# A Nyström attention, GLU and soft-MoE kernel on one Trainium2 core: idle products, the last soft-MoE's tiles and the prefetch ring changed

## The chip, the core and the metric

The kernel runs on one core of one Trainium2 chip. The metric is the device time of one execution in microseconds. The kernel before was timed in three runs: 731.29, 730.26 and 728.56 us, a median of 730.26 us. Times in rows are counted from the start of the profiled execution's span.

## What is computed

Three layers follow each other, all in float32 at the inputs and outputs. `B, H, S, D = 8, 8, 576, 64`, 4608 tokens of 512 features.

```python
# 1 Nystroem attention, per batch and head, 32 landmarks
A, Bm, C = softmax(q @ k_lm.T), softmax(q_lm @ k_lm.T), softmax(q_lm @ k.T)
Z = six Newton steps from Bm.T / (norm1 * norminf)
x = A @ Z @ C @ v
# 2 GLU
x = (silu(x @ w_gate) * (x @ w_val)) @ w_out
# 3 soft MoE, 8 experts with 4 slots each
logits = x @ phi                                   # (4608, 32)
d = softmax(logits, over tokens); slot_input = d.T @ x
for e in range(8):
    slot_out[e] = relu(slot_input[e] @ w1[e]) @ w2[e]
c = softmax(logits, over slots)
out = c @ slot_out
```

## The kernel before, in words

The whole work is written for one core with a tile framework that places instructions on the engines (PE, DVE, ACT, POOL, and SP for DMAs), follows the dependences of tiles, and orders each engine's instructions. The kernel walks over 8 batches. Each batch has 12 column blocks of the GLU (`unit`, line 880), and beside these the attention of the next batch (`attention`) and the soft-MoE of the batch before (`softmoe(b)`, line 778, a generator in steps) run in slots that a table of numbers gives.

`softmoe(b)` takes the batch's logits L from PSUM into the tile LT (128 x 160: 576 tokens as 4 x 144, so the last 32 columns are used on 64 partitions only). It finds the maximum over tokens of each slot (`cm`, a transpose `m_x` on PE, `gm`, `gmax`, `row`), spreads it with a product `m_y`, takes the exponential of LT with the sum of its rows (`dsum`), transposes LT to DN, spreads DN by four products `m_dr` (line 834) into DR, and multiplies DR with the GLU's result HB in 72 small products `m_d` (line 848), which four DVE operations add to Sacc. The running sum over tokens is `den`. A second copy of the logits, CN, becomes the softmax over slots.

For batch 7, the last, no GLU runs beside it. There `keep_warm` (line 770) puts products on PE whose result nobody reads: 3, 4, 2 and 2 of them (`WARM`, line 911) at four places, with LT or DN as stationary operand.

After the loop the tail (lines 1086 to 1212) follows: `m_s` transposes Sacc, `m_si` multiplies it with w_out (three tiles `wo`, read back from DRAM) to the experts' input SI, a transpose `m_sit` and twelve copies (lines 1119 to 1126, half on DVE, half on ACT) write it three times into the operands ZP, the first expert products `m_f` (line 1156) read w1, the second (line 1204) w2, in two halves `dh` of the columns, and `outputs` multiplies with c, evicts to buffers `ob` and stores.

The experts' weights are 32 tiles of 1 MB (0 to 15 of w1, 16 to 31 of w2), all loaded by SP in order into a ring of buffers `ffn_tags` (line 980): seven buffers `fw` in the space that the attention leaves at the end of batch 6 (`tail_loads`, line 1001), three parts of HB, six tiles `w0` to `w5` of the GLU's weights (of which `w0` to `w2` first hold `wo`), and three buffers `fx` in the space that the GLU leaves. That makes 20. The seven `fw` are loaded at the last slot of batch 6; tile 16 goes into a part of HB when m_d of batch 7 has read it, 17 to 19 into `w0` to `w2` as `m_si` reads them, and tile 20 and the following each into the buffer that a product has just read (`pump`).

Of the kernel before, what the change touches and what calls it, by code (L numbers as in the profile page):

```python
# [18 lines left out]
M = 32  # L19
# [36 lines left out]
def nystrom_softmoe_kernel(  # L56
# [49 lines left out]
    DN = cp.tile([128, 5, M], F32, name="DN")  # L106

    DR = cp.tile([128, 4, 5, M], F32, name="DR")
    dsum = cp.tile([128, 2], F32, name="dsum")
    gmax = cp.tile([1, M], F32, name="gmax")  # L110
# [658 lines left out]

    def keep_warm(x, n):  # L770

        m = psp.tile([128, 512], F32, tag="pg", name="warm", bufs=2)
        for _ in range(n):
            pe.matmul(m[:, 0:160], ident, x, start=True, stop=True)

    mb_t = []

    def softmoe(b):
        L = L_t[b]
        assert ("l", b, NJ - 1) in seq  # L780
        act.copy(LT[:, 0:128], L[:, 0:128])
        act.copy(LT[0:64, 128:160], L[0:64, 128:160])
        yield
        cm = smp.tile([128, 2], F32, tag="cm", name="cm")
        dve.tensor_reduce(cm[:, 0:1], LT[:, 0:128], axis=AX.X, op=ALU.max)
        dve.tensor_reduce(cm[0:64, 1:2], LT[0:64, 128:160], axis=AX.X, op=ALU.max)
        dve.tensor_tensor(out=cm[0:64, 0:1], in0=cm[0:64, 0:1], in1=cm[0:64, 1:2], op=ALU.max)
        c = CN[:, b]
# [4 lines left out]
        if b == nb - 1:  # L793
            keep_warm(LT, WARM[0])
        row = smp.tile([1, 4, M], F32, tag="row", name="row")
# [17 lines left out]
        yield  # L813
        in_order("exp", LT[:, 0:128], LT[:, 0:128], AF.Exp, bias=mb[:, 0:1], accum_out=dsum[:, 0:1])
        in_order("exp", LT[0:64, 128:160], LT[0:64, 128:160], AF.Exp, bias=mb[0:64, 0:1], accum_out=dsum[0:64, 1:2])
        if b == nb - 1:
            keep_warm(LT, WARM[1])
        al = smp.tile([128, 1], F32, tag="al", name="al")
# [4 lines left out]
        dve.transpose(DN, LT.rearrange("p (k r) -> p k r", r=32))  # L823
        ds_ = smp.tile([128, 1], F32, tag="ds", name="ds")
        if b:
            dve.tensor_tensor(out=ds_, in0=dsum[:, 0:1], in1=dsum[:, 1:2], op=ALU.add)
            dve.scalar_tensor_tensor(out=den, in0=den, scalar=al, in1=ds_, op0=ALU.mult, op1=ALU.add)
        else:
            dve.tensor_tensor(out=den, in0=dsum[:, 0:1], in1=dsum[:, 1:2], op=ALU.add)
        yield  # L830

        for g in range(4):
            m = psp.tile([128, 512], F32, tag="x", name="m_dr", bufs=3)
            pe.matmul(m[:, 0:160], msum[32 * g:32 * g + 32, :], DN[32 * g:32 * g + 32].rearrange("p k s -> p (k s)"),
                      start=True, stop=True)
            o = DR[:, g].rearrange("p k s -> p (k s)")
            act.copy(o, m[:, 0:160]) if g % 2 else dve.tensor_copy(o, m[:, 0:160])
        if b == nb - 1:
            keep_warm(DN.rearrange("p k s -> p (k s)"), WARM[2])
        yield  # L840
# [10 lines left out]
        if b == nb - 1:  # L851
            keep_warm(DN.rearrange("p k s -> p (k s)"), WARM[3])
        yield
# [56 lines left out]

    WARM = [3, 4, 2, 2]

# [4 lines left out]
    pool.memset(one, 1.0)  # L917
    for t in (LT, dsum):
        pool.memset(t, 0.0)
    load_qk(0, 0)  # L920
# [57 lines left out]
    last = nb - 1  # L978
    NW, NX = 7, 3
    ffn_tags = ([f"fw{i}" for i in range(NW)] + ["00", "01", "02", "w3", "w4", "w5"] + [f"fx{i}" for i in range(NX)]  # L980
# [5 lines left out]
    def wbuf(tag, name):  # L986
        if tag[:2] in ("fw", "fx"):
            return (fwp if tag[1] == "w" else fxp)[0].tile([128, 2048], F32, tag=tag, name=name)
        return big(tag, name) if tag[0] == "w" else part(int(tag[0]), int(tag[1]))
# [105 lines left out]
    ST, SI = misc[:, 1408:1792].rearrange("p (i x) -> p i x", i=3), misc[:, 1792:1920]  # L1095
    act.copy(ST, m[:, 0:384].rearrange("p (i x) -> p i x", i=3))
    rden = smp.tile([128, 1], F32, name="rden")
    dve.tensor_scalar(rden, m[:, 384:385], 1e-9, None, ALU.add)
# [19 lines left out]
    mz = m[:, 0:128].rearrange("p (c j g s) -> p c j g s", c=4, j=4, g=2)  # L1118
    for a in range(3):
        for g in range(2):  # L1120
            for z, c in ((ZP3, slice(0, 3)), (ZP1, slice(3, 4))):
                o = z[:, :, 4 * g:4 * g + 4, 8 * a + 4 * g:8 * a + 4 * g + 4]
                if g:
                    act.copy(o, mz[:, c, :, g, :])
                else:
                    dve.tensor_copy(o, mz[:, c, :, g, :])

    cT = {}

    def c_split(b):  # L1130

        if b % 2 == 0:
            cT[b // 2] = wbuf(ffn_tags[12 + b // 2], f"cT{b // 2}").bitcast(F32R)[:, 0:2 * S]
        c3 = misc[:, 768:1408].bitcast(F32R).rearrange("p (k j a x) -> p k j a x", k=5, j=4, a=4)
# [35 lines left out]

    free = ffn_tags[16:] + ffn_tags[0:4]
    nob = [0]
# [24 lines left out]
    for dh in range(2):  # L1197
        m = psp.tile([128, 512], F32, tag="pg", name="m_f2", bufs=2)
        for g in range(2):
            for r in range(4):  # L1200
# [6 lines left out]
                if dh == 0 and 4 * g + r < nb:  # L1207
                    c_split(4 * g + r)
        SR = fxp[0].tile([128, 256], F32R, name=f"SR{dh}")
        act.activation(SH, m[:, 0:256], AF.Copy, scale=hi_sign)  # L1210
# [58 lines left out]
```

## Time and profile before

| what | value |
|---|---|
| median of three runs | 730.26 us |
| lowest, highest | 728.56, 731.29 us |
| the profiled execution: its time | 733.54 us |
| its span, first to last instruction | 731.8 us |
| mean granted clock of PE | 0.954 of 2.4 GHz |
| busy: PE, DVE, ACT, POOL | 664.4, 513.5, 318.1, 114.7 us |
| DMA: moved, mean rate | 105.04 MB, 144 GB/s |

A busy time is an average over stages that have different limits. The page cuts the span into 40 slices of 18.3 us; the windows cut it where a stage begins. PEclk is the share of PE's full clock that was granted. A granted clock of 0.50 is 1.2 GHz, of 1.00 it is 2.4 GHz.

### The profile page before, as it was taken

How to read it: one execution, taken by the hardware profiler on the slowest of the kernel's cores; microseconds unless marked ns; L12 is line 12 of the kernel's file. 1: busy time of each engine (PE TensorE's matmuls, PEld its weight loads, DVE VectorE, ACT ScalarE, POOL GpSimd, SP SyncE). 2: the span in 40 equal slices, each digit the busy share in tenths (PEclk: the TensorE clock that was granted, in tenths of full speed). 3: DMA queues.
4: the chain of work that ended last, by engine and by line, in shares of the span. 5: the costliest groups of instructions: out<-in, count | busy, mean ns of one | idle time of the engine just before them, and what ended most of it. 6: DMA issues, size and time to landing. Idle time of an engine off the chain costs nothing.

```text
span 731.8 us, 18736 instructions
## 1 busy us (share of the span) xinstructions
PE 664.4 (91%) x7749; PEld 488.8 (67%) x7749; DVE 513.5 (70%) x1247; ACT 318.1 (43%) x821; POOL 114.7 (16%) x125
## 2 busy tenths in 40 slices
PE   5687878999899999999999999999999998898990
PEld 1564657776587777767776777787768777662560
DVE  5999998878765896689578856985786655520351
ACT  2566766436433643364237333633453342301440
POOL 0544464302100120021012001200120000010000
PEclk9797898999999999999999999999999999979995
DMA  8687555204210330034011401240101699549999
GB/s 295 213 312 291 206 197 203 93 2 130 67 66 2 130 105 29 22 111 131 1 66 67 131 1 66 67 130 2 65 2 60 212 267 303 174 146 335 348 364 330
DMA packets 59990, 105.04 MB, mean 144 GB/s; under 512 B 3968, under 2 KB 29696, under 8 KB 58368
## 3 DMA queue, kind: packets, MB, share of 16 engines
q1 hardware_dynamic: 59904, 103.84, 43.5%
q8 instruction: 61, 1.00, 0.6%
q14 instruction: 25, 0.20, 0.1%
HBM read 91.24 MB, written 12.58 MB: 142 GB/s over the span
## 4 chain that ended last, share of the span: by engine, by line
PE 72%; DVE 14%; DMA 4%; ACT 4%; issue 2%; POOL 1%; SPq 0%; DVEq 0%; ACTq 0%; POOLq 0%
PE pg L877 20%; PE pv L877 18%; PE g L709 6%; PE l L761 5%; PE m_d L848 4%; PE m_n L636 3%; PE m_f L1156 2%; PE m_f L1204 2%; PE m_a L528 2%; DMA q<-in_qT_dram 2%; DMA out_dram<-ob 1%; DMA HB<-in_w_cat_dram 1%; PE m_c L528 1%; DVE bd L311 1%; PE m_v L617 1%
## 5 line engine op out<-in xcount | busy, mean ns | idle before, releaser
L301 ACT ACTIVATE u<-pg 128x288 f32<-128x288 f32 x174 | 71.5, 412 | 156.5 <-PE pg L877 146.8
L906 DVE TENSOR_TENSOR hT<-u,pv 128x288 f32<-128x288 f32 x162 | 72.9, 451 | 54.8 <-PE pv L877 48.6
L877 PE MATMUL pg<-EH,GH 128*128 128x288 f32 x384 | 97.9, 332 | 2.2 <-ACT GH L732 2.2
L877 PE MATMUL pv<-EH,GH 128*128 128x288 f32 x384 | 92.3, 314 | 3.9 <-DVE hT L906 3.9
L877 PE MATMUL pg<-EH,GL 128*128 128x288 f32 x384 | 87.5, 302 | 2.2 <-issue 2.0
L746 DVE TENSOR_TENSOR GL<-g,GH 128x512 fp32r<-128x512 f32 (+1 forms) x114 | 63.2, 580 | 34.1 <-ACT GH L732 33.7
L877 PE MATMUL pg<-EL,GH 128*128 128x288 f32 x384 | 84.8, 302 | 0.0
L877 PE MATMUL pv<-EH,GL 128*128 128x288 f32 x384 | 84.3, 296 | 0.0
L877 PE MATMUL pv<-EL,GH 128*128 128x288 f32 x384 | 83.4, 298 | 0.0
L877 PEld LDWEIGHTS pg<-EH,GH 128*128 128x128 f32 x384 | 61.0, 192 | 24.3 <-issue 19.0
L877 PEld LDWEIGHTS pv<-EH,GH 128*128 128x128 f32 x384 | 62.2, 190 | 21.4 <-issue 16.6
L766 DVE STREAM_TRANSPOSE HB<-hT 128x576 f32<-128x576 f32 x96 | 74.0, 770 | 1.6 <-POOL hT L902 0.2
L732 ACT CAST GH<-g 128x512 fp32r<-128x512 f32 (+1 forms) x114 | 51.7, 506 | 51.7 <-PE g L709 51.6
L877 PEld LDWEIGHTS pg<-EH,GL 128*128 128x128 f32 x384 | 63.5, 191 | 4.9 <-issue 3.6
L877 PEld LDWEIGHTS pg<-EL,GH 128*128 128x128 f32 x384 | 62.6, 192 | 2.5 <-issue 2.5
L877 PEld LDWEIGHTS pv<-EH,GL 128*128 128x128 f32 x384 | 62.8, 190 | 0.0
L877 PEld LDWEIGHTS pv<-EL,GH 128*128 128x128 f32 x384 | 62.7, 191 | 0.0
L709 PE MATMUL g<-w,WB 64*32 64x512 f32 (+1 forms) x976 | 59.7, 515 | 1.6 <-ACT HB L728 0.8
L761 PE MATMUL l<-hT,P_sb 128*32 128x128 f32 (+1 forms) x768 | 48.5, 301 | 0.6 <-DVE hT L906 0.6
L761 PEld LDWEIGHTS l<-hT,P_sb 128*32 128x32 f32 x768 | 16.1, 108 | 40.6 <-issue 17.6
L682 POOL TENSOR_TENSOR AN<-AN,mxA 128x576 f32<-128x576 f32 x16 | 18.4, 1167 | 152.9 <-DVE mxA L681 136.8
L848 PE MATMUL m_d<-HB,DR 32*32 32x384 f32 x1152 | 41.3, 513 | 0.0
(259 smaller groups left out, 1068.5 us busy)
## 6 DMA issues: line engine op xcount, KB each, us to landing
k<-in_kT_dram SPq DMA_DIRECT2D x52, 288.0 KB, 3.9
ffn<-in_w_dram SPq DMA_DIRECT2D x13, 1024.0 KB, 9.2
ffn<-in_w_dram SPq DMA_DIRECT2D x24, 512.0 KB, 8.8
HB<-in_w_cat_dram SPq DMA_DIRECT2D x8, 1024.0 KB, 6.1
v<-in_v_dram SPq DMA_DIRECT2D x8, 1024.0 KB, 5.6
q<-in_qT_dram SPq DMA_DIRECT2D x28, 288.0 KB, 3.5
HB<-in_w_out_dram SPq DMA_DIRECT2D x12, 512.0 KB, 5.3
out_dram<-ob SPq DMA_DIRECT2D x6, 1024.0 KB, 10.0
```

The source lines that it names most:

```text
L301: i = act.activation(*a, **kw)
L528: pe.matmul(ms[r][32 * hp:32 * hp + 32, 0:HALF], lm[64 * r:64 * r + 64, hp, :], qk_t[nm, b, hp][64 * r:64 * r + 64, HALF * half:HALF * hal ...
L636: pe.matmul(m[:, 96 * q:96 * q + 96], bd[:, q, :], RV[:, q, :], start=True, stop=True)
L682: lambda q: pool.tensor_tensor(out=AN[q], in0=AN[q], in1=bc[q], op=ALU.subtract),
L709: pe.matmul(gs[r][32 * hp:32 * hp + 32, 0:256 * n].rearrange("p (u f) -> p u f", u=n), WB[b % 2][64 * r:64 * r + 64, hp, :], w[64 * r:64 * ...
L732: act.copy(H_, g)
L746: dve.tensor_tensor(out=GL, in0=g, in1=GH, op=ALU.subtract)
L761: pe.matmul(L[32 * c:32 * c + 32, 0:32 * k], P_sb[:, j, :], main[:, 0:k, c, :], start=j == 0, stop=j == NJ - 1)
L766: dve.transpose(HB[b % 2][:, S * j:S * j + S].rearrange("p (t r) -> p t r", r=32), hT[:, 0:S].rearrange("p (t r) -> p t r", r=32))
L848: pe.matmul(ms[a][32 * g:32 * g + 32, 0:384].rearrange("p (j f) -> p j f", j=NJ), DR[32 * a:32 * a + 32, g, k, :], hb[32 * a:32 * a + 32, ...
L877: pe.matmul(ps[:, 0:HALF], G_t[b, j, q, sel_][h], e[:, q, ts_], start=n == 0, stop=n == 5)
L906: dve.tensor_tensor(out=o, in0=u, in1=pv[:, 0:HALF], op=ALU.mult)
```

## The change

It has seven edits.

1. `keep_warm` multiplies the constants (the identity with a part of `cst`) in place of LT or DN, into the PSUM buffer of the logits. The counts are 3, 5, 2, 2, and a fifth place, after the copy of `m_s`, has 2.
2. The corner of LT that holds no tokens is set to -3e38 by POOL in each `softmoe`, so that one maximum and one exponential run over the whole tile; `dsum` has one column, and the two additions with it are gone.
3. DR has no tile of its own any more; it lies in the unused end of the other HB.
4. The ring of weight tiles has eight `fw` buffers, 21 in all.
5. The copies into ZP write all three replicas at once, from an operand that is read three times: four on DVE, then four on ACT.
6. SR lies in buffer `w2` and no longer in the space of `fx`.
7. The buffers of the transposed c and of the outputs are taken from other places of the ring.

```diff
-    DR = cp.tile([128, 4, 5, M], F32, name="DR")
-    dsum = cp.tile([128, 2], F32, name="dsum")
+    dsum = cp.tile([128, 1], F32, name="dsum")
...
-    def keep_warm(x, n):
-        m = psp.tile([128, 512], F32, tag="pg", name="warm", bufs=2)
+    def keep_warm(n):
+        m = psp.tile([128, 512], F32, tag="l", name="warm")
         for _ in range(n):
-            pe.matmul(m[:, 0:160], ident, x, start=True, stop=True)
+            pe.matmul(m[:, 0:160], ident, cst[:, 128:288], start=True, stop=True)
...
-        yield
-        cm = smp.tile([128, 2], F32, tag="cm", name="cm")
-        dve.tensor_reduce(cm[:, 0:1], LT[:, 0:128], axis=AX.X, op=ALU.max)
-        dve.tensor_reduce(cm[0:64, 1:2], LT[0:64, 128:160], axis=AX.X, op=ALU.max)
-        dve.tensor_tensor(out=cm[0:64, 0:1], in0=cm[0:64, 0:1], in1=cm[0:64, 1:2], op=ALU.max)
+        pool.memset(LT[64:128, 128:160], -3e38)
+        yield
+        cm = smp.tile([128, 1], F32, tag="cm", name="cm")
+        dve.tensor_reduce(cm, LT, axis=AX.X, op=ALU.max)
...
-        in_order("exp", LT[:, 0:128], LT[:, 0:128], AF.Exp, bias=mb[:, 0:1], accum_out=dsum[:, 0:1])
-        in_order("exp", LT[0:64, 128:160], LT[0:64, 128:160], AF.Exp, bias=mb[0:64, 0:1], accum_out=dsum[0:64, 1:2])
+        in_order("exp", LT, LT, AF.Exp, bias=mb[:, 0:1], accum_out=dsum)
...
-            dve.tensor_tensor(out=ds_, in0=dsum[:, 0:1], in1=dsum[:, 1:2], op=ALU.add)
-            dve.scalar_tensor_tensor(out=den, in0=den, scalar=al, in1=ds_, op0=ALU.mult, op1=ALU.add)
+            dve.scalar_tensor_tensor(out=den, in0=den, scalar=al, in1=dsum, op0=ALU.mult, op1=ALU.add)
...
+        DR = spare[(b + 1) % 2][:, 0:640].rearrange("p (g k s) -> p g k s", g=4, k=5)
...
-    WARM = [3, 4, 2, 2]
+    WARM = [3, 5, 2, 2, 2]
...
-    NW, NX = 7, 3
+    NW, NX = 8, 3
...
     act.copy(ST, m[:, 0:384].rearrange("p (i x) -> p i x", i=3))
+    keep_warm(WARM[4])
...
-    for a in range(3):
-        for g in range(2):
-            for z, c in ((ZP3, slice(0, 3)), (ZP1, slice(3, 4))):
-                o = z[:, :, 4 * g:4 * g + 4, 8 * a + 4 * g:8 * a + 4 * g + 4]
+    for g in range(2):
+        for z, c in ((ZP3, slice(0, 3)), (ZP1, slice(3, 4))):
+            for i in range(c.stop - c.start):
+                o = z[:, i, 4 * g:4 * g + 4, 0:24].rearrange("p j (a x) -> p j a x", a=3)[:, :, :, 4 * g:4 * g + 4]
+                v_ = mz[:, c.start + i, :, g, :].unsqueeze(2).to_broadcast([128, 4, 3, 4])
                 if g:
-                    act.copy(o, mz[:, c, :, g, :])
+                    act.copy(o, v_)
                 else:
-                    dve.tensor_copy(o, mz[:, c, :, g, :])
+                    dve.tensor_copy(o, v_)
...
-            cT[b // 2] = wbuf(ffn_tags[12 + b // 2], f"cT{b // 2}").bitcast(F32R)[:, 0:2 * S]
+            cT[b // 2] = wbuf(ffn_tags[11 + b // 2], f"cT{b // 2}").bitcast(F32R)[:, 0:2 * S]
...
-    free = ffn_tags[16:] + ffn_tags[0:4]
+    free = ffn_tags[15:20] + ffn_tags[0:3]
...
-        SR = fxp[0].tile([128, 256], F32R, name=f"SR{dh}")
+        if dh == 0:
+            SR2 = wbuf(ffn_tags[20], "SR")
+        SR = SR2[:, 256 * dh:256 * dh + 256].bitcast(F32R)
```

The framework moves instructions with it. These are PE's rows of the last soft-MoE, from the last logits to the products m_s, before (`cst` holds the constants, `wo` the w_out tiles):

```order
L761 MATMUL l<-hT,P_sb 32x160 x2
L761 MATMUL l<-hT,P_sb 32x128 x2
L774 MATMUL warm<-LT,cst 128x160 x3
L792 MATMUL m_x<-cst,cm 1x128
L803 MATMUL m_y<-one,row 128x1
L774 MATMUL warm<-LT,cst 128x160 x4
L834 MATMUL m_dr<-DN,cst 128x160 x4
L774 MATMUL warm<-DN,cst 128x160 x2
L848 MATMUL m_d<-HB_87,DR 32x384 x72
L774 MATMUL warm<-DN,cst 128x160 x2
L1090 MATMUL m_s<-cst,Sacc 128x32 x12
```

And of the change, the same stretch:

```order
L759 MATMUL l<-hT,P_sb 32x160 x2
L759 MATMUL l<-hT,P_sb 32x128 x2
L772 MATMUL warm<-cst 128x160 x2
L790 MATMUL m_x<-cst,cm 1x128
L772 MATMUL warm<-cst 128x160 x4
L801 MATMUL m_y<-one,row 128x1
L772 MATMUL warm<-cst 128x160 x6
L830 MATMUL m_dr<-DN,cst 128x160 x4
L844 MATMUL m_d<-HB_86,HB_85 32x384 x72
L772 MATMUL warm<-cst 128x160 x2
L1085 MATMUL m_s<-cst,Sacc 128x32 x12
```

Twelve idle products stand ahead of m_dr where seven stood; none is left between m_dr and m_d. The products with the count of the fifth place are the two behind m_d.

DVE's rows of the same soft-MoE, from the sum over CN to the copies into DR, before:

```order
L864 TENSOR_REDUCE mxc<-CN 128x5
L865 TENSOR_SCALAR mxc<-mxc 128x5
L866 RECIPROCAL mxc<-mxc 128x5
L867 TENSOR_TENSOR CN<-CN,mxc 128x160
L823 STREAM_TRANSPOSE DN<-LT 128x160
L826 TENSOR_TENSOR ds<-dsum 128x1
L827 SCALAR_TENSOR_TENSOR den<-den,al,ds 128x1
L837 COPY DR<-m_dr 128x160 x2
```

And of the change:

```order
L860 TENSOR_REDUCE mxc<-CN 128x5
L861 TENSOR_SCALAR mxc<-mxc 128x5
L820 STREAM_TRANSPOSE DN<-LT 128x160
L822 SCALAR_TENSOR_TENSOR den<-den,al,dsum 128x1
L862 RECIPROCAL mxc<-mxc 128x5
L863 TENSOR_TENSOR CN<-CN,mxc 128x160
L833 COPY HB_85<-m_dr 128x160 x2
```

DN has moved ahead of two operations on CN, and one small addition is gone.

SP's rows of batch 7 and of the end of the loop, from the tiles in HB's first three parts to the first load that follows m_si, before (`ffn` is a weight tile, one or two DMAs each; the DMA of 128x4x512 is a tile of w1, a pair of 128x4x256 one of w2):

```order
L967 DMA HB_86<-in_w_dram 128x4x512 x3
L967 DMA ffn_8379<-in_w_dram 128x4x512
L967 DMA ffn_8493<-in_w_dram 128x4x512
L967 DMA ffn_8591<-in_w_dram 128x4x512
L967 DMA ffn_8610<-in_w_dram 128x4x512
L967 DMA ffn_8612<-in_w_dram 128x4x512
L967 DMA ffn_8614<-in_w_dram 128x4x512
L975 DMA HB_87<-in_w_dram 128x4x256 x2
L975 DMA ffn_8830<-in_w_dram 128x4x256 x2
```

And of the change:

```order
L962 DMA HB_85<-in_w_dram 128x4x512 x3
L962 DMA ffn_8352<-in_w_dram 128x4x512
L962 DMA ffn_8466<-in_w_dram 128x4x512
L962 DMA ffn_8564<-in_w_dram 128x4x512
L962 DMA ffn_8583<-in_w_dram 128x4x512
L962 DMA ffn_8585<-in_w_dram 128x4x512
L970 DMA ffn_8587<-in_w_dram 128x4x256 x2
L970 DMA HB_86<-in_w_dram 128x4x256 x2
L970 DMA ffn_8804<-in_w_dram 128x4x256 x2
```

The last of the three `fx` buffers now takes tile 16, the part of HB that waits for m_d takes tile 17, and the first load behind m_si is tile 18 where it was 17. Seven loads of w1 tiles ahead of these rows have become eight.

## Rows read from the trace of the kernel before

**Rows 1.** The page's DMA line: busy share in 40 slices of the span, in tenths.

```profile
DMA  8687555204210330034011401240101699549999
```

**Rows 2.** Windows of the tail: stretch, length, busy of each engine, PEclk, DMA share, GB/s.

```profile
634.30:638.30 4.00, 1.54 (x9) 1.16 (x9) 3.14 (x16) 2.80 (x9) 0.00 (x0) 0.90 0.96 221
638.30:640.75 2.45, 2.44 (x9) 2.11 (x9) 0.80 (x4) 0.05 (x1) 0.00 (x0) 0.50 1.02 376
640.75:644.25 3.50, 3.10 (x13) 2.04 (x12) 0.56 (x2) 0.58 (x2) 0.00 (x0) 0.50 0.94 356
644.25:647.75 3.50, 3.50 (x83) 1.95 (x97) 0.00 (x0) 0.00 (x0) 0.00 (x0) 0.50 0.07 28
...
650.10:654.40 4.30, 3.86 (x32) 3.60 (x31) 2.90 (x6) 0.33 (x2) 2.74 (x3) 1.00 0.70 212
654.40:656.90 2.50, 2.14 (x41) 1.85 (x45) 0.32 (x2) 0.47 (x1) 0.00 (x0) 0.54 0.17 55
...
718.10:729.60 11.50, 0.00 (x0) 0.00 (x0) 0.00 (x0) 0.00 (x0) 0.00 (x0) 0.50 1.05 362
...
656.90:729.60 72.70, 53.34 (x568) 28.98 (x560) 19.44 (x50) 20.06 (x46) 1.72 (x7) 0.88 1.06 347
```

**Rows 3.** Timeline, batch 7's soft-MoE: start, duration, instruction, idle before it and releaser.

```profile
634.71 1.08 PE L774 MATMUL warm<-LT,cst 128*128 128x160 f32 x6 [0.47 <-ACT LT L782]
...
635.63 0.27 PE L792 MATMUL m_x<-cst,cm 128*1 128x128 f32 x1
...
636.83 0.35 PE L803 MATMUL m_y<-one,row 1*128 1x1 f32 x2 [0.93 <-DVE row L800]
...
637.46 0.40 ACT L301 ACTIVATE LT<-LT,mb 128x128 f32<-128x128 f32 x1 [1.14 <-DVE mb L805]
...
638.31 2.50 PE L774 MATMUL warm<-LT,cst 128*128 128x160 f32 x8 [1.14 <-ACT LT L301]
638.50 0.34 DVE L823 STREAM_TRANSPOSE DN<-LT 128x160 f32<-128x160 f32 x1
...
640.75 0.91 PE L834 MATMUL m_dr<-DN,cst 32*128 32x160 f32 x6
...
643.00 0.29 ACT L837 COPY DR<-m_dr 128x160 f32<-128x160 f32 x1 [0.98 <-PE m_dr L834]
```

**Rows 4.** Timeline, the soft-MoE of batch 6 beside the GLU of batch 7: m_dr and its last copy.

```profile
595.61 0.55 PE L834 MATMUL m_dr<-DN,cst 32*128 32x160 f32 x6
...
597.13 0.29 ACT L837 COPY DR<-m_dr 128x160 f32<-128x160 f32 x1 [0.19 <-PE m_dr L834]
```

**Rows 5.** Chain in order of time: m_d of batch 6's soft-MoE, the exponential and m_d of batch 7's.

```profile
600.85 4.25 PE m_d L848 x141
...
637.46 0.81 ACT LT L301 x4
...
644.32 5.75 PE m_d L848 x136
```

**Rows 6.** Timeline of SP: the experts' loads as they are issued.

```profile
572.62 8.86 SPq L967 DMA_DIRECT2D ffn<-in_w_dram  x6
...
656.92 26.75 SPq L975 DMA_DIRECT2D ffn<-in_w_dram  x20
```

**Rows 7.** Windows ahead of the tail, columns as above.

```profile
624.00:628.00 4.00, 4.00 (x47) 3.19 (x46) 2.08 (x5) 1.47 (x4) 0.00 (x0) 1.00 0.07 26
628.00:634.00 6.00, 5.38 (x51) 4.68 (x49) 2.84 (x7) 1.24 (x3) 0.00 (x0) 1.00 0.54 176
```

**Rows 8.** Timeline: the first copies into ZP, and the first expert product.

```profile
660.17 0.29 DVE L1126 COPY HB<-m_sit 128x48 f32<-128x48 f32 x2 [4.91 <-PE m_sit L1116]
...
661.76 7.72 PE L1156 MATMUL m_f<-ffn,HB 128*32 128x512 f32 x56 [1.70 <-DVE HB L1126]
```

**Rows 9.** Chain in order of time: q's loads in batch 1, and a stall of PE in batch 7.

```profile
189.73 4.14 DMA q<-in_qT_dram
...
608.67 1.95 issue
```

More of the change, by code (lines that the diff above doesn't have):

```diff
@@ L793, in softmoe @@
         if b == nb - 1:
-            keep_warm(LT, WARM[0])
+            keep_warm(WARM[0])
         row = smp.tile([1, 4, M], F32, tag="row", name="row")
@@ L813, in softmoe @@
         yield
-        in_order("exp", LT[:, 0:128], LT[:, 0:128], AF.Exp, bias=mb[:, 0:1], accum_out=dsum[:, 0:1])
-        in_order("exp", LT[0:64, 128:160], LT[0:64, 128:160], AF.Exp, bias=mb[0:64, 0:1], accum_out=dsum[0:64, 1:2])
+        in_order("exp", LT, LT, AF.Exp, bias=mb[:, 0:1], accum_out=dsum)
         if b == nb - 1:
-            keep_warm(LT, WARM[1])
+            keep_warm(WARM[1])
         al = smp.tile([128, 1], F32, tag="al", name="al")
@@ L823, in softmoe @@
         dve.transpose(DN, LT.rearrange("p (k r) -> p k r", r=32))
-        ds_ = smp.tile([128, 1], F32, tag="ds", name="ds")
         if b:
-            dve.tensor_tensor(out=ds_, in0=dsum[:, 0:1], in1=dsum[:, 1:2], op=ALU.add)
-            dve.scalar_tensor_tensor(out=den, in0=den, scalar=al, in1=ds_, op0=ALU.mult, op1=ALU.add)
+            dve.scalar_tensor_tensor(out=den, in0=den, scalar=al, in1=dsum, op0=ALU.mult, op1=ALU.add)
         else:
-            dve.tensor_tensor(out=den, in0=dsum[:, 0:1], in1=dsum[:, 1:2], op=ALU.add)
+            dve.tensor_copy(den, dsum)
         yield
+        DR = spare[(b + 1) % 2][:, 0:640].rearrange("p (g k s) -> p g k s", g=4, k=5)
         for g in range(4):
@@ L838, in softmoe @@
         if b == nb - 1:
-            keep_warm(DN.rearrange("p k s -> p (k s)"), WARM[2])
+            keep_warm(WARM[2])
         yield
@@ L851, in softmoe @@
         if b == nb - 1:
-            keep_warm(DN.rearrange("p k s -> p (k s)"), WARM[3])
+            keep_warm(WARM[3])
         yield
@@ L917, in nystrom_softmoe_kernel @@
     pool.memset(one, 1.0)
-    for t in (LT, dsum):
-        pool.memset(t, 0.0)
+    pool.memset(LT, 0.0)
     load_qk(0, 0)
```

## The prediction

> **What bounds the kernel now.** I read the page first, then the windows, the order of time on each engine, and the chain of waits. The page's DMA line [rows 1] says that the program has two parts. After the first fifth of the span and up to its last quarter the DMA engines have little to do, and PE is what everything waits for. In the last tenth they are busy all the time. Cut into stages [rows 2], the end reads so: from 656.9 to 729.6 us the DMA engines are at a share of 1.06 and move 347 GB/s, and for the last 11.5 us of it PE, DVE, ACT and POOL do nothing at all. So the end is a drain: it comes when the bytes that are left at 656.9 have been moved. Two things set it, how many bytes these are and when the drain starts. It starts when SP issues the loads at 656.92 [rows 6]: these wait until the products m_si have read the first `wo` tile, since they go into the same buffers. Up to there PE's own chain runs alone, and the DMA engines are idle for most of 644 to 657 (shares of 0.07 in the middle of m_d and of 0.17 at m_si [rows 2]).
>
> What PE does in this stretch is the last batch's soft-MoE. Its clock is at the lower of its two levels (1.2 GHz, granted 0.50) from about 637.5 to 647.8 us and again after 654.6, and at the upper (2.4 GHz) between [rows 2]. Before the first fall PE was busy for 1.54 of 4.0 us. The idle products meant to fill such holes read LT and DN, so they run only after LT or DN is there, and stand in the way of what needs the same data: the four after the exponential take 2.50 us at the low clock, and hold m_dr back until 640.75 although DN was written by 638.84 [rows 3].
>
> **The change, part by part.**
>
> *The eighth prefetch tile.* One more load of 1024 KB (1.049 MB) goes out at the end of batch 6, beside six such loads of 8.86 us of issuing [rows 6], and everything behind it shifts by one: after m_si there are 14 tiles left to load where there were 15. The drain is 1.049 MB shorter, at 347 GB/s [rows 2] **3.0 us**. The early load costs 3.0 us of DMA time before the tail. Its cover is the idle time at 624 to 628 (share 0.07) and 628 to 634 (0.54) [rows 7], 3.7 + 2.8 = 6.5 us; without that cover it would push the three tiles that load from 633 on, and these are not needed until the first expert product is under way. SP's queue: the twelve `wo` loads move behind it, and they are needed at 655. Nothing else waits there.
>
> *Idle products on constants.* The order now has two before m_x, four before m_y and six before m_dr, none after m_dr. At the high clock three take 0.92 us from the first one's start to m_x, 0.31 each [rows 3]. So m_x starts 0.3 us earlier (634.71 + 0.62), four more end at 636.85, and m_y starts as now (636.83): DVE's chain to `row` gains 0.1 to 0.2 us from the single maximum, and PE takes it back. m_y ends at 637.18 and six products at 637.18 + 1.86 = 639.04. DN needs less than that: one exponential of 160 columns in place of two (0.81 us with their accumulator reads [rows 5] become some 0.45, estimated from the first, 0.40 [rows 3]), and DVE takes DN ahead of two small operations; it would be there at about 638.3. So m_dr starts at 639.0 in place of 640.75: **-1.7 us**.
>
> *m_dr to m_d.* From 640.75 to 644.25 now: 3.5 us, with two idle products in it, all at 0.50 [rows 2, 3]. In batch 7's earlier soft-MoE the same four products and copies at the high clock took from 595.61 to 597.42, 1.8 us [rows 4]. The two products are gone from there: **-1.7 us**, if the clock holds.
>
> *m_d.* 5.75 us now, of which 3.4 at 0.50; one batch earlier 4.25 us [rows 5], in a stretch without any idle time of PE: **-1.5 us**, if the clock holds.
>
> *The clock.* No row shows PE with these holes filled. From the end of the logits to m_dr, 634.3 to 639.0, it would be busy 12 x 0.31 + 0.27 + 0.35 = 4.3 of 4.7 us, against 1.54 of the 4.0 us in which the clock fell now. Nearest are the dense stretches, where it stayed up; so I take it as held.
>
> *m_s and m_si.* PE's small products m_s (32 columns each) ran at 1.00 and the clock fell right after them [rows 2]. Five us earlier the fall can come inside them: 3.86 us of PE's work there, at worst all of it slower. Bounds: -0.5 (a little less of m_si at 0.50) and +1.7; I take **+0.8**, between them, because after m_d the rows show the same thin work as now. The drain thus starts 1.7 + 1.7 + 1.5 - 0.8 = **4.1 us** earlier.
>
> *The expert operand.* Twelve copies in turns between DVE and ACT become four on each. The first m_f waits 1.6 us from 660.17 on [rows 8] and would wait one copy, so PE gains about 1.3 us there. I cost it at nothing: by then three tiles (9 us of DMA time) are in the queue and the DMA engines set the pace. Without that cover it would be worth its 1.3 us. The two products after m_d, the cleared corner of LT on POOL, and the tags of the outputs cost nothing: PE waits for DVE's sums there, and POOL is idle.
>
> *The earlier batches.* The same edits run in batches 1 to 6 beside the GLU, where PE is nearly always busy, so saved DVE and ACT time buys nothing. One place is different: in batch 1, PE waits behind a chain that ends with the loads of q [rows 9], and the new order of DVE frees one k slot earlier. Bounds -1.3 (one of the three loads less in the chain's 4.14 us) and +0.5 (ACT puts an exponential ahead of an activation there); I take **-0.4**.
>
> Sum: -3.0 - 4.1 - 0.4 = -7.5 us. Against the profiled execution, 733.54 us, that is 726.0; it lies 3.3 us above the median shown, 730.26, and I see no row that says why, so the same 7.5 us come off the median: **722.8, said as 723.0 us**.
>
> **The rivals.**
>
> *The clock falls anyway.* The rows show that PE at the low clock stayed there through 638.3 to 644.25, although it was busy 5.54 of 5.95 us with products of the very same kind [rows 2]. If it falls at 637.5 as now, the six products take 0.31 + 5 x 0.62 us, m_dr starts at 640.6, and only the two products that no longer stand before m_d are saved (1.0 us at the low clock, 0.55 us once it is up again). 730.26 - 3.0 - 0.55 - 0.4 = **726.3 us**. The Trainium skill speaks for this one ("TensorE: Matmul & The Clock Gate", section "HAM oscillation — how this bites in real kernels"): it lays the fall to waits between bursts that are much longer than any here. By that rule the holes of about 1 us in [rows 3] would not be what brought the clock down, and filling them would not hold it; the sum by it is the 726.3 above, by the rows the 723.0. Against it: the fall did come after just these holes.
>
> *The tile buys nothing.* If what ends the program is not the bytes but the last output's way through PE, ACT and DVE, the drain's 3.0 us stay and 730.26 - 4.1 - 0.4 = **725.8 us**. Against it: 11.5 us without any engine at work at a DMA share of 1.05 [rows 2].
>
> *Slower: the idle products become the path.* Twelve stand before m_dr now, seven before. If the clock is down already when they begin (634.7), they cost 12 x 0.62 = 7.5 us; with m_x and m_y m_dr starts near 643.2, 2.4 us late, and m_d at 645.8, 1.5 us late; if m_d then stays at the low clock to its end, 8.1 us in place of 5.8, it ends 3.8 us late. 730.26 + 3.8 - 3.0 = **731.1 us**. The point that decides is the granted clock at 634.7: it was 1.00 before, so this needs a fall one stage sooner. A stall of PE in heavy DMA traffic like the 1.95 us at 608.67 [rows 9] would add to it.
>
> **How the numbers follow.** About 0.5%, 3.65 us, is what a measurement of this kernel can tell from no change: faster is below 726.6, slower above 733.9. Forecast 0.65; clock falls 0.17; tile buys nothing 0.10; idle products the path 0.05; something else, on either side, 0.03. Nearly all of the first, and a little over half of the second and third, lie under 726.6: faster 0.79, same 0.17, slower 0.04. The range: 723.0 less 1.3 (m_s), 0.9 (batch 1) and about 1.5 (the runs lay within 728.56 to 731.29) gives 719.3, said as 719.0; upward it takes in the clock that falls, 726.3, with some of the same scatter, 727.5.
>
> **What would show it.** Right: a granted clock of 1.00 from 634 to past m_d; m_dr starting at most 2 us after m_y ends; m_d in about 4.3 us; SP's loads after m_si starting about 4 us sooner, counted from the last logits; then some 69.7 us of drain in place of 72.7 at an unchanged rate. Wrong: a clock of 0.50 within m_dr or m_d (first rival); a drain of equal length (second); m_dr later than 6.5 us after the logits (third).

## The result: 720.84 us in place of 730.75 us

Beside each other the changed kernel took 720.84 us (median of 4 runs, 719.78 to 723.72) and the kernel before 730.75 us (4 runs, 728.56 to 731.29): ratio 0.9863, 95% interval 0.9828 to 0.9899. A later comparison gave 0.9851 (0.9820 to 0.9882). The kernel before had medians of 730.75 to 733.48 us in the four comparisons of this document, so kernels of different comparisons are set beside each other by their ratios. The forecast was 723.0 us, its range 719.0 to 727.5. The profiled execution took 720.9 us with a span of 719.1 (before: 733.54 and 731.8).

The page's DMA line answers to [rows 1]. The busy last part is there again:

```profile
DMA  8687645304220431034012402240211399669999
```

The windows of the tail answer to [rows 2] (length, busy of PE, PEld, DVE, ACT, POOL, PEclk, DMA share, GB/s). They run from the last logits to m_dr in two steps, then m_dr, m_d, m_s with m_si's wait, the first half of m_si, and the drain:

```profile
627.65:631.90 4.25, 3.72 (x22) 3.00 (x23) 2.99 (x14) 2.57 (x7) 0.00 (x0) 1.00 0.99 298
631.90:633.10 1.20, 1.14 (x8) 0.74 (x6) 0.54 (x4) 0.00 (x0) 0.00 (x0) 1.00 0.92 283
633.10:634.53 1.43, 1.02 (x10) 0.60 (x9) 0.56 (x2) 0.29 (x1) 0.00 (x0) 1.00 1.08 312
634.53:639.27 4.74, 4.74 (x146) 2.84 (x145) 0.41 (x1) 0.29 (x1) 0.32 (x1) 1.00 0.71 235
639.27:643.68 4.41, 4.00 (x32) 3.61 (x32) 2.89 (x7) 0.80 (x2) 2.75 (x3) 0.98 0.67 223
643.68:645.67 1.99, 1.99 (x40) 1.85 (x44) 0.30 (x2) 0.00 (x0) 0.00 (x0) 0.50 0.10 32
...
645.67:717.00 71.33, 51.90 (x568) 28.64 (x560) 19.14 (x48) 19.83 (x44) 1.72 (x7) 0.91 1.03 339
```

The clock is at 1.00 to the end of m_d, where it was 0.50 from the idle products ahead of m_dr until well into m_d [rows 2]. The timeline of the soft-MoE of batch 7 answers to [rows 3] (start, duration, instruction, idle before it and releaser):

```profile
630.33 0.38 PE L801 MATMUL m_y<-one,row 1*128 1x1 f32 x2
...
630.63 2.55 PE L772 MATMUL warm<-cst 128*128 128x160 f32 x12
...
631.57 0.35 DVE L820 STREAM_TRANSPOSE DN<-LT 128x160 f32<-128x160 f32 x1
...
633.11 0.55 PE L830 MATMUL m_dr<-DN,cst 32*128 32x160 f32 x6
```

DN is written at 631.92, and m_dr starts 1.2 us later, when the six idle products (12 rows) are done. SP's loads after m_si start at 645.67 (timeline of SP), against 656.92 [rows 6]:

```profile
645.67 16.06 SPq L970 DMA_DIRECT2D ffn<-in_w_dram  x12
```

Cut at the end of the last logits (634.24 us before, 627.59 after) and at that first load, the 12.7 us between the two spans lie so: 6.65 us ahead of the last logits, 4.6 between these and the load (22.68 against 18.08), and 1.45 in the drain, from the load to the end of the span (74.88 against 73.43). The prediction had 0.4, 4.1 and 3.0. The medians are only 9.9 us apart: the profiled execution of before lay 2.8 us above its median, so these parts are those of one pair of executions, and their sum is larger than the gain.

### The profile page after: what moved, and what is told of

Same layout as the page of the kernel before. It is cut to its first block, busy times and chain, and to the rows that moved or that the text cites. A ratio compares the mean times of both kernels' runs of the same rounds, so it can differ in the third digit from the quotient of the medians.

```text
span 719.1 us, 18723 instructions
## 1 busy us (share of the span) xinstructions
PE 661.3 (92%) x7755; PEld 488.0 (68%) x7755; DVE 510.8 (71%) x1222; ACT 315.5 (44%) x803; POOL 115.7 (16%) x132
## 4 chain that ended last, share of the span: by engine, by line
PE 67%; DVE 17%; DMA 5%; ACT 5%; issue 3%; POOL 2%; SPq 0%; DVEq 0%; POOLq 0%; ACTq 0%
PE pg L873 20%; PE pv L873 17%; PE g L707 6%; PE l L759 5%; PE m_d L844 4%; PE m_n L634 3%; PE m_f L1153 2%; PE m_a L526 2%; DMA out_dram<-ob 1%; DVE w L179 1%; DMA HB<-in_w_dram 1%; DVE bd L309 1%; PE m_c L526 1%; DMA ffn<-in_w_dram 1%; DVE HB L179 1%
## 5 line engine op out<-in xcount | busy, mean ns | idle before, releaser
L844 PE MATMUL m_d<-HB,HB 32*32 32x384 f32 x1152 | 40.7, 491 | 0.3 <-DVE GL L744 0.3
```

What stands on the lines that cost most here:

```text
L844: pe.matmul(ms[a][32 * g:32 * g + 32, 0:384].rearrange("p (j f) -> p j f", j=NJ), DR[32 * a:32 * a + 32, g, k, :], hb[32 * a:32 * a + 32, ...
```

## The experiments

Each kernel ran beside the kernel before. The table gives the ratio to it with its interval and, from the profile, the end of the last logits, the first load after m_si counted from there, and the drain from that load to the end of the span (us; two values: two profiles).

| kernel | ratio | logits end | load | drain |
|---|---|---|---|---|
| before | 1 | 634.2, 634.0 | 22.68, 22.65 | 74.9, 75.4 |
| padded tile alone | 0.9953 (0.9930 to 0.9976) | 630.7 | 22.22 | 76.5 |
| soft-MoE edits alone | 0.9937 (0.9910 to 0.9964) | 629.3 | 21.05 | 76.1 |
| idle products alone | 0.9964 (0.9939 to 0.9989) | 634.8 | 18.34 | 76.5 |
| changed, seven tiles | 0.9897 (0.9863 to 0.9931) | 630.3 | 18.09 | 76.4 |
| changed | 0.9863 and 0.9851 | 627.6, 632.2 | 18.08, 18.08 | 73.4, 73.5 |
| changed, no idle products | 0.9853 (0.9819 to 0.9888) | 628.5 | 19.21 | 72.6 |
| changed, old operand copies | 0.9853 (0.9825 to 0.9881) | 628.0 | 17.23 | 73.7 |
| changed, four idle | 0.9821 (0.9786 to 0.9856), 0.9833 (0.9803 to 0.9863) | 627.5, 629.0 | 16.38, 17.21 | 72.3, 72.3 |
| changed, two idle | 0.9841 (0.9813 to 0.9870) | 628.3 | 16.94 | 72.1 |
| changed, idle in m_s | 0.9867 (0.9831 to 0.9904) | 628.2 | 17.30 | 72.2 |

The end of the logits differs by up to 4.8 us between profiles with the same order of the batches; one part of that is a stall of PE in batch 7 ("pg <- issue" in the table of waits), 0.4 to 3.0 us long whatever the kernel.

**The soft-MoE's own edits, alone.** The question is where 6.65 us went ahead of the tail.

```diff
-    DR = cp.tile([128, 4, 5, M], F32, name="DR")
+        pool.memset(LT[64:128, 128:160], -3e38)
-        dve.tensor_reduce(cm[:, 0:1], LT[:, 0:128], axis=AX.X, op=ALU.max)
...
+        dve.tensor_reduce(cm, LT, axis=AX.X, op=ALU.max)
-        in_order("exp", LT[:, 0:128], LT[:, 0:128], AF.Exp, bias=mb[:, 0:1], accum_out=dsum[:, 0:1])
-        in_order("exp", LT[0:64, 128:160], LT[0:64, 128:160], AF.Exp, bias=mb[0:64, 0:1], accum_out=dsum[0:64, 1:2])
+        in_order("exp", LT, LT, AF.Exp, bias=mb[:, 0:1], accum_out=dsum)
+        DR = spare[(b + 1) % 2][:, 0:640].rearrange("p (g k s) -> p g k s", g=4, k=5)
```

> The kernel before with only the soft-MoE's own edits: the padded tile with one maximum and one exponential, one column of dsum, and DR in a spare buffer. Theory (as predicted): batch 1's loads of q give 0.4 us and the shorter exponential at most another 0.4 us in the tail, so 730 us against 730.75; PE's wait in batch 1 for the chain behind q (3.65 us before) stays between 2.4 and 4.2 us. Rival: the win of 3.8 us that the two profiles show in batch 1 belongs to these edits; then PE's wait there is under 1 us and the time is 726 to 727 us.

729.23 us against 733.48, ratio 0.9937, so 4.6 us (2.6 to 6.6 by the interval): the rival's size, six times the theory's. The wait of PE in batch 1 is down to 0.3 us, as the rival had it.

**The padded tile alone** tells the two edits apart. It is the diff above, but these two lines stay as before:

```diff
     DR = cp.tile([128, 4, 5, M], F32, name="DR")
-        DR = spare[(b + 1) % 2][:, 0:640].rearrange("p (g k s) -> p g k s", g=4, k=5)
```

> The kernel before with only the padded tile: one maximum, one exponential, one column of dsum; DR stays a tile of its own. Theory now: the 4.9 us won ahead of the last logits come from the order of DVE in batch 1, where this edit brings the first reduction of k ahead of two wide transposes, frees a buffer and so lets a load of q go out 7 us sooner. Then PE's wait in batch 1 for hT is under 0.6 us here, and the time is that of the two soft-MoE edits together, 0.994 of before. Rival: the wait hangs on the place of DR; then it is over 3 us here and the time 0.998 to 1.000 of before.

Ratio 0.9953, the wait 0.4 us: the padded tile does it. The rows show how, by the order of DVE. The timeline of batch 1 of the kernel before (first profile), on DVE and SP:

```profile
187.35 0.73 DVE L322 TENSOR_REDUCE ks<-k 128x32 f32<-128x576 f32 x1
188.30 2.06 DVE L322 TENSOR_REDUCE ks<-k 128x32 f32<-128x576 f32 x3
...
188.12 2.60 SPq L154 DMA_DIRECT2D q<-in_qT_dram  x4
```

What PE waited for there, from the waits of the same profile (total, times, longest):

```profile
PE pv L877 <- DVE hT L906: 3.7, 1, 3.7
```

The same timeline of the kernel with the padded tile alone:

```profile
180.34 0.70 DVE L322 TENSOR_REDUCE ks<-k 128x32 f32<-128x576 f32 x1
186.33 2.06 DVE L322 TENSOR_REDUCE ks<-k 128x32 f32<-128x576 f32 x3
...
181.07 7.68 SPq L154 DMA_DIRECT2D q<-in_qT_dram  x4
```

And PE's wait there:

```profile
PE pv L873 <- DVE hT L902: 0.4, 1, 0.4
```

The first reduction of k comes 7 us sooner and frees a buffer, so the first load of q goes out 7 us sooner; the other three reductions are 2.0 us sooner, and their loads with them. DVE works in order: hT stood behind the reductions of q that wait for these loads, and PE waits for hT.

**The kernel before, a second time.**

> The kernel before once more, for a second profile. If the first one is typical: PE waits over 3 us in batch 1 for hT, the last logits end near 631 to 634 us (the stall of PE in batch 7 near 605 us lay between 0.4 and 3.0 us in the profiles so far), m_d takes 5.7 us at a clock that is 0.50 in its first half, the loads after m_si start 22.7 us after the last logits. The drain from there to the end of the span: 74.9 us again if a later start makes it shorter, 76.0 to 76.5 as in the kernels with part of the change if the first profile had a lucky drain.

733.76 us; the wait in batch 1 is 3.2 us, the last logits end at 633.97, and the load starts 22.65 us later: the first profile was typical. The drain is 75.4, between the two expectations.

**The idle products alone.**

```diff
-    def keep_warm(x, n):
+    def keep_warm(n):
-            pe.matmul(m[:, 0:160], ident, x, start=True, stop=True)
+            pe.matmul(m[:, 0:160], ident, cst[:, 128:288], start=True, stop=True)
-    WARM = [3, 4, 2, 2]
+    WARM = [3, 5, 2, 2, 2]
```

> The kernel before with only the idle products on constants (three before m_x, four before m_y, seven before m_dr, none after it). Theory: granted clock 1.00 from the last logits to the end of m_d; m_dr starts about 5.8 us after the last logits end (seven products instead of six end later than in the changed kernel), m_d 4.7 us; SP's loads after m_si 4.0 us sooner counted from the last logits, 726.7 us. Rival 1, the clock falls anyway: 0.50 within m_d, about 730 us. Rival 2, the changed kernel held the clock because of the shorter exponential and not by the idle products: the clock falls before m_dr as in the kernel before. Up to batch 6 the instructions are those of the kernel before: if PE's wait in batch 1 is near 3.7 us again it belongs to that code, if it is under 1 us the profile of before was an outlier there.

The windows of this kernel from the last logits to m_dr, of m_dr, and of m_d (columns as above):

```profile
634.83:641.10 6.27, 5.63 (x31) 4.28 (x31) 4.00 (x19) 2.85 (x9) 0.00 (x0) 1.00 0.93 276
641.10:642.52 1.42, 1.02 (x10) 0.60 (x9) 0.56 (x2) 0.29 (x1) 0.00 (x0) 1.00 1.04 395
642.52:647.26 4.74, 4.74 (x145) 2.77 (x144) 0.41 (x1) 0.29 (x1) 0.00 (x0) 1.00 0.49 185
```

The clock stays at 1.00 with the two exponentials of before, so both rivals fall; the load starts 4.3 us sooner. But the ratio, 0.9964, is 2.6 us and not 4.0. The interval (0.8 to 4.5 us) does not rule 4.0 out; the profile shows what was lost, a drain of 76.5 us in place of 74.9 and 75.4.

**Seven tiles.**

```diff
-    NW, NX = 8, 3
+    NW, NX = 7, 3
...
-            SR2 = wbuf(ffn_tags[20], "SR")
+        SR = fxp[0].tile([128, 256], F32R, name=f"SR{dh}")
```

SR and the buffers of the transposed c and of the outputs go back with it (the lines of the latter are left out here).

> The changed kernel with seven prefetch tiles in place of eight, the tags of the late buffers as before. Theory (as predicted): the drain is longer by one tile, 1.049 MB at 347 GB/s, 3.0 us: 723.8 us. By the two profiles (loads after m_si to the end of the span 74.9 us before, 73.4 after) the tile gave only 1.5 us: 722.3 us. Rival, the tile buys nothing: 720.8 us. If the slow start of the drain in the changed kernel (109 to 168 GB/s from 649.2 to 651.2) comes from the eighth tile, it is gone here and the drain starts at over 280 GB/s within 3 us.

The drain is 76.4 us against 73.4 and 73.5: the tile is worth 3.0 us, as forecast; by the ratios, 0.9897 here and 0.9863 and 0.9851 for the changed kernel, it is 2.5 to 3.4 us, though the intervals of these ratios overlap. What looked like half of it in the first two profiles is another loss, which the kernel with seven tiles has too. Windows of 4 us from the first load after m_si on; the kernel before:

```profile
656.92:660.92 4.00, 2.64 (x65) 2.10 (x57) 0.34 (x3) 0.64 (x3) 0.00 (x0) 0.86 0.69 184
660.92:664.92 4.00, 3.16 (x16) 0.79 (x20) 0.53 (x4) 0.55 (x4) 0.00 (x0) 0.57 0.98 318
```

With seven tiles:

```profile
648.38:652.38 4.00, 3.13 (x73) 2.24 (x69) 0.55 (x4) 0.60 (x3) 0.00 (x0) 0.90 0.56 164
652.38:656.38 4.00, 4.00 (x42) 1.17 (x36) 0.00 (x0) 0.37 (x3) 0.00 (x0) 1.00 0.94 264
```

The changed kernel:

```profile
645.67:649.67 4.00, 3.14 (x69) 2.29 (x65) 0.55 (x4) 0.41 (x2) 0.00 (x0) 0.85 0.57 165
649.67:653.67 4.00, 4.00 (x44) 1.30 (x40) 0.00 (x0) 0.56 (x4) 0.00 (x0) 1.00 0.79 232
```

In its first 8 us the drain of before moves 4 x (184 + 318) = 2.01 MB, the others 1.71 and 1.59. At 348 GB/s these 0.30 and 0.42 MB are 0.9 and 1.2 us. After that all three run at 346 to 358 GB/s up to the outputs.

SP's rows differ together with this loss. The first two loads are the two halves of a tile. To issue the second one takes SP 0.50 us in the kernel before:

```profile
657.34 0.50 SPq L975 DMA_DIRECT2D ffn<-in_w_dram  x1
```

In the changed kernel it takes 1.60 us:

```profile
646.08 1.60 SPq L970 DMA_DIRECT2D ffn<-in_w_dram  x1
```

Over the fourteen profiles this duration parts the long drains from the short. It is 0.50 or 0.51 us in the kernel before (twice), the one without idle products, those with four (twice) and two, and the one with idle products in m_s; it is 1.18 to 1.75 us in the other seven. With one tile, 3.0 us, added where eight are loaded ahead, the drains of the first group are 74.9 to 75.6 us, those of the second 76.1 to 76.7. In all seven of the second group a load of instructions (16 KB, queue q8 in the view of the DMAs) starts within 1 us of the first load, but it does so in two of the first group too; so what holds SP up is not shown.

**No idle products at all.**

```diff
-    WARM = [3, 5, 2, 2, 2]
+    WARM = [0, 0, 0, 0, 0]
```

> The changed kernel without any idle product (the counts are all zero). Theory: the clock falls in the soft-MoE of batch 7, m_dr can start 1.2 us earlier (as DN is written) but m_dr to m_d takes 2.4 us in place of 1.4, m_d 5.8 to 8 us in place of 4.7, and m_si runs wholly at 0.50; loads after m_si 1 to 4 us later counted from the last logits, 721.8 to 725 us. Rival, the clock does not depend on these products: it is 1.00 in m_d, m_dr starts 1.2 us earlier, 719.6 us.

The windows of this kernel, from the last logits to m_dr, of m_dr, and of the two parts of m_d:

```profile
628.51:632.51 4.00, 0.62 (x3) 0.37 (x3) 2.93 (x14) 2.57 (x7) 0.00 (x0) 0.95 0.96 290
632.51:634.80 2.29, 1.78 (x10) 1.08 (x12) 1.07 (x5) 0.29 (x1) 0.00 (x0) 0.50 1.02 277
634.80:638.50 3.70, 3.70 (x84) 2.35 (x97) 0.00 (x0) 0.29 (x1) 0.00 (x0) 0.50 1.00 321
638.50:641.10 2.60, 2.60 (x78) 1.69 (x57) 0.20 (x1) 0.00 (x0) 0.14 (x1) 0.92 0.22 72
```

PE's rows there, with the holes ahead of m_x, m_y and m_dr in brackets:

```profile
629.49 0.27 PE L790 MATMUL m_x<-cst,cm 128*1 128x128 f32 x1 [0.99 <-DVE cm L785]
630.93 0.35 PE L801 MATMUL m_y<-one,row 1*128 1x1 f32 x2 [1.17 <-DVE row L798]
632.64 0.91 PE L830 MATMUL m_dr<-DN,cst 32*128 32x160 f32 x6 [1.36 <-DVE den L822]
```

The clock falls, and m_d takes 6.36 us (634.75 to 641.10) in place of 4.74. Yet m_dr starts 4.1 us after the last logits in place of 5.5, so the load is only 1.1 us later, and the drain is 0.9 us shorter: from the last logits to the end it is 91.8 us against 91.5.

**The changed kernel again.**

> The changed kernel once more, beside the kernel without idle products of the first set (0.9853 of before) and for a second profile. If the idle products are worth what the sum of the prediction gave them in the tail (the loads after m_si started 1.1 us sooner with them than without), the ratio is 0.983 to 0.985; if they are worth nothing in the end, it is 0.985 to 0.987, that of the kernel without them. The drain from the first load after m_si to the end of the span: 73.4 us again if its slow second window (232 GB/s from 4 to 8 us after that load) belongs to the code, 72.4 if that window is one of the things that differ from run to run.

Ratio 0.9851, and 0.9853 without the idle products: what they gain at the load does not show at the end, though an interval of 0.3% to either side could hide 1.1 us. The profiles say where it goes: the drain without them is of the short group, that of the changed kernel of the long one. The second profile repeats the slow start of the drain (73.5 us, 235 GB/s in the second window).

**Four idle products before m_dr, none after m_d**, two comparisons.

```diff
-    WARM = [3, 5, 2, 2, 2]
+    WARM = [3, 5, 0, 0, 2]
```

The two products of the fifth place now stand ahead of m_dr, which makes four there.

> The changed kernel with four idle products before m_dr in place of six and none after m_d. Theory: the six end 1.2 us after DN is written and hold m_dr back; with four, m_dr starts 0.6 us earlier (about 4.9 us after the last logits), the clock stays at 1.00 to the end of m_d, the loads after m_si start 0.6 us sooner, 720.3 us on the scale of the changed kernel's 720.8. Rival: four are too few, the clock falls in m_d (5 to 6 us in place of 4.7), no gain. Second rival: the gain at the loads comes and is given back in the drain, as between the changed kernel and the one without idle products: same time.

> The kernel with four idle products before m_dr again, beside the three others, to tell it from the changed kernel (0.9863 and 0.9851 of before in its two comparisons; this one 0.9821). If the gain at the loads, 1.7 us, reaches the end, the ratio is 0.981 to 0.983 again; if it is the scatter of one comparison, 0.984 to 0.986.

m_dr starts 4.65 us after the last logits, the clock is 1.00 to the end of m_d, the loads start 0.9 and 1.7 us sooner, and the drain is 1.1 us shorter as well, so none of it is given back. From the last logits to the end the two profiles have 88.7 and 89.5 us, the changed kernel 91.5 and 91.6. The medians are 720.45 us beside 722.78 for the changed kernel, and 720.39 in the second comparison. The second ratio, 0.9833, lies nearer to the first than to the changed kernel's, but the intervals overlap (0.9803 to 0.9863 here, 0.9820 to 0.9882 there), so the runs alone do not settle it.

**Two idle products before m_dr,** none after m_d.

```diff
-    WARM = [3, 5, 2, 2, 2]
+    WARM = [3, 3, 0, 0, 2]
```

> The changed kernel with two idle products before m_dr in place of six, and none after m_d. Theory: m_dr can start only when DN is written, 4.3 us after the last logits; the two end at 3.9, so m_dr starts at 4.4 (4.65 with four, 5.5 with six) after a hole of 0.5 us; the clock stays at 1.00 to the end of m_d, and the time is 0.2 to 0.5 us below that with four. Rival: the hole is enough for the clock to fall in m_d (over 5.5 us in place of 4.7), and the loads after m_si start later than 16.4 us after the last logits.

As the theory had it, m_dr starts 4.4 us after the last logits, behind a hole of 0.53 us, and m_d takes 4.74 us at a clock of 1.00. The 0.2 to 0.5 us that it expected to gain on four do not show: the ratio is 0.9841 beside 0.9833 and 0.9821, and differences of this size are below what the runs can tell.

**Idle products among m_s.** The counts are those of the kernel with four (3, 5, 0, 0, 2), but the two of the fifth place now stay behind m_s, so two are left before m_dr; and m_s gets:

```diff
+        pe.matmul(mw[:, 0:160], Sacc[:, a, 0:128], cst[:, 128:288], start=True, stop=True)
```

> The changed kernel with two idle products before m_dr, one of 160 columns with Sacc as stationary operand after every three of the twelve small products m_s, and two after m_s. In all kernels so far the clock is 0.50 in the first two thirds of m_si, after m_s (2.87 us of 32-column products), m_si 4.3 to 4.5 us. Theory: the thin products are what brings it down; with four wide ones among them the clock stays at 1.00, m_si takes 2.6 to 3.2 us, m_s 3.6 to 4.1; loads after m_si 0 to 0.8 us sooner, 0 to 1 us in the end. Rival: the clock falls as before, m_si 4.3 us or more, and the four products only cost their 1 us.

The windows of m_s and of m_si in this kernel:

```profile
639.47:643.62 4.15, 4.15 (x35) 4.12 (x35) 2.09 (x4) 0.00 (x0) 2.03 (x3) 1.00 0.76 230
644.30:647.13 2.83, 2.83 (x98) 2.63 (x97) 0.19 (x2) 0.00 (x0) 0.00 (x0) 1.00 0.21 33
```

The same two in the kernel with two idle products:

```profile
639.64:642.71 3.07, 3.07 (x27) 3.05 (x27) 2.09 (x4) 0.00 (x0) 2.03 (x3) 1.00 0.63 193
643.27:647.60 4.33, 4.33 (x96) 3.83 (x96) 0.31 (x2) 0.00 (x0) 0.00 (x0) 0.64 0.43 145
```

The clock holds and m_si takes 2.83 us in place of 4.33, as theory had it. That the wide products did it is not shown: this is one profile, and in the kernel below the clock held through m_si without them. The wide products cost 1.1 us in m_s and the two after it about 0.1 more, and the first loads wait for a third of m_si, not for its end. No gain: 0.9867, with 0.9841 inside its interval.

**The old operand copies** in the changed kernel.

```diff
-    for g in range(2):
-        for z, c in ((ZP3, slice(0, 3)), (ZP1, slice(3, 4))):
-            for i in range(c.stop - c.start):
...
+    for a in range(3):
+        for g in range(2):
+            for z, c in ((ZP3, slice(0, 3)), (ZP1, slice(3, 4))):
+                o = z[:, :, 4 * g:4 * g + 4, 8 * a + 4 * g:8 * a + 4 * g + 4]
```

> The changed kernel with the expert operand written by twelve copies in turns of DVE and ACT, as before. Theory (as predicted): the first expert product starts 1.2 us later after m_sit, and the DMA engines set the pace, so the time is that of the changed kernel, 0.985 of before. Rival: PE's late start delays the release of the first buffers and the drain; 1.2 us more, 0.9867. If the slow second window of the drain (232 to 235 GB/s in the changed kernel, 318 to 322 before) comes from these copies or from the earlier expert products, it is back above 300 here, and the drain 1 us shorter.

Ratio 0.9853: as forecast, no difference at the end that the interval (0.3% to either side, 2 us) lets one see, although the first expert product starts 1.7 us after m_sit's end and not 0.4. The drain is as long (73.7 us), its second window 241 GB/s, so its slow start does not come from the new copies. The load is 0.85 us sooner than in the changed kernel (17.23 us): here the clock stayed at 1.00 through m_si, which took 2.83 us, and fell to 0.58 in the first 4 us of the expert products instead.

## Why the prediction was right, and where it was not

The total came within the range, but two terms were mis-sized, in opposite directions. The earlier batches gave 4.9 us more than was forecast, where the range had room for 0.9; a longer drain took some of that back. That the time still lies within the range is in part luck. The parts measured alone do account for the whole: by the ratios the soft-MoE's edits are worth 4.6 us, the idle products 2.6 and the tile 2.5 to 3.4, together 9.7 to 10.6, and the whole change 10.0 and 10.9 in its two comparisons.

*The earlier batches, "I take -0.4": the step that failed.* The profiles with the padded tile end the last logits at 627.5 to 632.2 us, mean 629.1 over eleven; the three with the old order at 634.0 to 634.8, mean 634.4. That is 5.3 us. About 3.0 of it is the wait of PE in batch 1, 3.2 to 3.7 us with the old order and at most 0.5 with the new; the rest is not assigned. The place and the chain were named, but the bound of -1.3 assumed one load less in a chain of 4.14 us. It left out that hT is queued on DVE behind the reductions of q, and that the other three reductions of k move up as well, so nearly the whole wait went.

*The eighth tile, -3.0: right.* 76.4 against 73.4 and 73.5 us. The rival in which the tile buys nothing is refuted by these drains; the ratios alone would not do it. (The ring of before has four parts of HB, three filled early and one after m_d: 7 + 4 + 6 + 3 = 20 buffers.)

*The drain starts earlier, -4.1: right at its start, not at its end.* The load is 4.6 us sooner. By parts: m_dr -1.0 in place of -1.7, because the six idle products took 2.5 us and not 1.86; m_dr to m_d -2.1 in place of -1.7; m_d, 4.74 us, -1.1 in place of -1.5; m_s and m_si +0.8 forecast, but m_si took 4.36 us as before, and from the end of m_d to the load it is 0.4 us shorter. What failed is the assumption that the drain has a fixed length at an unchanged rate: its window is 71.3 us at 339 GB/s, not 69.7 at 347. Before, the drain is 74.9 and 75.4 us; with part of the change and the same bytes it is 76.1 to 76.5, so 1.0 to 1.4 us are given back, most of them at its start. This is not the price of a sooner start: with four or two idle products the load is 5.4 to 6.3 us sooner than before, and the drain is 72.1 to 72.3 us, that of before less the tile. The loss goes with SP's slow second issue, as shown above; what causes it stays open. Neither the tile, the copies nor the idle products alone bring it, since the kernel with the padded tile alone has it too.

*The clock falls anyway: refuted.* It was 1.00 through m_d in every profile with the holes filled, and 0.50 in the first part of m_d in those without. In the kernel without idle products it fell after three holes of 0.99 to 1.36 us, one after another, and in the kernel before after holes of 0.47 to 1.14 us [rows 3]. The rule of the Trainium skill ("TensorE: Matmul & The Clock Gate", section "HAM oscillation — how this bites in real kernels") behind that rival, which lays the fall to long waits between bursts, does not cover this case: no hole in these stretches was longer than 1.36 us.

But the clock is not what most of the gain hangs on. Of the 4.6 us at the load, 3.5 are there in the changed kernel without any idle product too, since the idle products of before had also held m_dr back, by 1.9 us after DN, and had stood between m_dr and m_d. Holding the clock with six adds only 1.1 us, because they hold m_dr back again; with four or two it adds 2.0 to 2.8. In the end the six show nothing (0.9853 without them, 0.9863 and 0.9851 with them), and the four and two 0.9 to 2.3 us by ratios whose intervals overlap.

*Slower, by the idle products on the path.* It did not come, but its mechanism is there in small: m_dr waited 1.2 us for them, and started 2.4 us after m_y's end where at most 2 was forecast.

*The operand copies at nothing: right,* as far as the interval tells.

## What to carry to other kernels

Idle products that hold a clock belong on constants, and no more of them than end when the awaited operand is there: with six m_dr waited 1.2 us, with four 0.3 us, with two not at all, and the clock held all the same. An edit that takes a few operations off an in-order engine can move others past each other in every earlier stage, so compare the order there too, and price the whole wait of whoever stands behind, not one link of its chain. Where a drain of transfers ends the program, bytes taken from it counted in full here. A sooner start did so in some kernels and lost up to 1.4 us in others, so look at the drain's first microseconds, and at how long its first issues take, before a gain at its start is counted as one at its end.

## What was not expected of the hardware

- Twelve products of 32 columns, with PE's rows busy for 3.07 of 3.07 us, were followed by a clock of 0.50 in m_si; with one product of 160 columns after every third it stayed at 1.00. It is no fixed rule, and one profile each does not make the wide products the cause: in the kernel with the old copies, whose instructions are the same up to there, m_si ran at the high clock too (2.83 us) and the clock fell in the first expert product.
- Transfers that were out did not fill the DMA engines: from 4 to 8 us into the drain the changed kernel moved 232 and 235 GB/s at a share of 0.79 in the first profile, the kernel before 318 and 322. All the long drains have a second load that took SP 1.18 us or more to issue, all the short ones one of 0.50 or 0.51 us.
